# One gate-weight transfer, the last rows in column halves, adds and stores given to GpSimd: a change to the start and the end of a fused attention and gated-MLP kernel

## Chip, cores, metric

One core of a Trainium2 chip runs the kernel. The metric is the device time of one execution in microseconds. A figure quoted for a kernel is the median of its runs. The profile is of one execution, and its span is about 1.8 us shorter than that execution's time.

## The reference, cut to what matters

```python
xn = layernorm(A_x)                                  # 2048 rows of 640
q  = (xn @ wq) -> 32 heads of 192;  k, v = last 512 positions of the caches
s  = softmax(q k^T / sqrt(192)) v  -> 6144 columns;  s = s @ wo
g  = silu((sigmoid(xn @ w_gate) * (xn @ w_up)) @ w_down)
return A_x + s * g                                   # bf16, 2048 x 640
```

## The kernel before

The rows are taken in 4 blocks of 512, the heads in 8 groups of 4, so there are 32 units (a group and a block). At the start, the first block's tiles of 128 rows are normalised and transposed on TensorE while the first gate and up weights arrive. TensorE runs the matmuls of tile 0, with the transposes of tile 1 in the middle:

```python
load_x(0, 1)                                 # rows 0-127, sync queue
load_x(1, 1)
load_f(nc.scalar, wg_sb, wg_r, 0, 4, 0, 3)   # gate weights, piece 1 (384 KB), activation queue
load_f(nc.sync,   wg_sb, wg_r, 0, 4, 3, NCD) # gate weights, piece 2 (256 KB), sync queue
load_f(nc.scalar, wu_sb, wu_r, 0, 4, 0, 3)   # up weights, piece 1
load_x(2, 1)
load_f(nc.sync,   wu_sb, wu_r, 0, 4, 3, NCD)
load_x(3, 1)
```

At the end, the last group's projection of a row tile is multiplied by the gate `g`, added to the kept sum `acc` (which already holds `A_x` plus the other groups' part times `g`), and stored:

```python
for cc in range(GC):                         # 6 steps, 512 + 128 columns each
    for d0, d1 in ((0, 512), (512, D)):
        nc.tensor.matmul(wide(k)[:, d0:d1], ...)
if g == NG - 1:
    o_sb = fin.tile([P, D], F32, name="o_sb", bufs=2)
    nc.vector.tensor_tensor(o_sb[:], wide(k)[:, 0:D], gate[:, t, :], ALU.mult)
    r_sb = gate[:, t, :]
    parts = ((0, D),) if out_eng is not None else ((0, 384), (384, D))
    for i, (d0, d1) in enumerate(parts):
        nc.vector.tensor_tensor(r_sb[:, d0:d1], o_sb[:, d0:d1], acc[:, t, d0:d1], ALU.add)
        eng = out_eng or (nc.scalar, nc.sync)[i]
        eng.dma_start(of[t * P:(t + 1) * P, d0:d1], r_sb[:, d0:d1])
# ... the last units, u = NU - 2:
# project(u - 2, ...), project(u - 1, ...) with stores on nc.sync, between score matmuls
# values and transposes (by DMA, sync queue) of u and u + 1
# project(u, q, order[q], nc.sync);  project(u + 1, q, order[q], nc.scalar if q < 3 else None)
```

The softmax here doesn't subtract the row's maximum and nothing guards it: scores larger than these inputs give would overflow.

## Time and profile before

| | before |
|---|---|
| median of three runs | 928.17 us (927.81 to 928.33) |
| the profiled execution | 929.19 us, span 927.4 us |
| TensorE busy | 919.2 us, 99% |

The page's busy table and the chain that ended last, of the kernel before (the chain names, for each share of the span, the work that had to finish before the next could go on):

```profile
PE 919.2 (99%) x8004; PEld 547.2 (59%) x8004; DVE 467.2 (50%) x736; ACT 302.8 (33%) x333; POOL 126.0 (14%) x152
...
PE 97%; DMA 1%; DVE 1%; SPq 0%; issue 0%; ACT 0%; DVEq 0%; ACTq 0%
```

TensorE is the bound almost everywhere. What is not TensorE lies at the two ends. The timeline of the kernel before, at the start (columns: start in us, duration, engine, line, operation, output and inputs, count, and in brackets the idle time before it and what ended it):

```profile
6.29 1.16 PE L300 MATMUL bank<-xnT,wg_sb 128*128 128x128 bf16 x12
...
8.44 0.62 PE L300 MATMUL bank<-xnT,wg_sb 128*128 128x128 bf16 x8 [0.99 <-DMA wg_sb<-in_B_w_gate_dram]
9.29 0.49 DVE L198 BATCH_NORM_STATS2 st<-x_sb 128x6 f32<-128x320 bf16 x1 [2.22 <-DMA x_sb<-in_A_x_dram]
...
9.50 0.84 PE L300 MATMUL bank<-xnT,wu_sb 128*128 128x128 bf16 x12 [0.44 <-DMA wu_sb<-in_B_w_up_dram]
...
10.19 0.45 PE L230 MATMUL bank<-ident,xn 128*128 128x128 bf16 x5
```

Twelve gate matmuls run on the first piece; TensorE then waits for the second, and again for the up weights. The transposes of the second tile (L230) mark the end of this load-bound stretch. The timeline of the kernel before, at the end:

```profile
908.67 1.79 PE L457 MATMUL bank<-wo_last,oT 128*128 128x512 bf16 x12
...
911.03 11.58 PE L457 MATMUL bank<-wo_last,oT 128*128 128x512 bf16 x84 [0.57 <-DMA oT<-o_st]
...
922.13 0.83 DVE L466 TENSOR_TENSOR gate<-o_sb,acc 128x640 bf16<-128x640 f32 x1
922.87 0.82 DVE L461 TENSOR_TENSOR o_sb<-bank,gate 128x640 f32<-128x640 f32 x1
923.79 0.90 DVE L466 TENSOR_TENSOR gate<-o_sb,acc 128x384 bf16<-128x384 f32 x2
924.71 0.33 SPq L468 DMA_DIRECT2D out_dram<-gate  x1
```

The chain of waits at the start, of the same trace, goes through the first up piece and the matmuls that use it:

```profile
1.68 7.78 DMA wu_sb<-in_B_w_up_dram
...
9.50 0.84 PE bank L300 x12
```

At the end, the second row tile waits 0.57 us for its transpose. VectorE needs 0.82 us to multiply and 0.83 us to add a row, against 1.63 us of TensorE work.

### The profile page before, as it was taken

To read this page: it belongs to the slowest core of one execution; us is meant where nothing else is said; L and a number is where in the kernel's file an instruction comes from. 1 tells how busy PE (TensorE), PEld (TensorE's weight loads), DVE (VectorE), ACT (ScalarE), POOL (GpSimd) and SP (SyncE) were. 2 spreads that over 40 slices of the span, in tenths; PEclk is the share of its full clock that TensorE was granted. 3 is DMA by queue.
4 is the path that set the end of the run, shared out by engine and by line. 5 is a ranking of instruction groups with operands and counts; after the bars stand their busy time and mean duration, and the time that the engine had idled before them with its cause. 6 is when DMAs were issued, how large, how long until landed. Compare 5 with 4: busy or idle time off the path is not lost.

```text
span 927.4 us, 18043 instructions
## 1 busy us (share of the span) xinstructions
PE 919.2 (99%) x8004; PEld 547.2 (59%) x8004; DVE 467.2 (50%) x736; ACT 302.8 (33%) x333; POOL 126.0 (14%) x152
## 2 busy tenths in 40 slices
PE   8999999999999999999999999999999999999997
PEld 6445454465756565656565656566666656565665
DVE  5452522444645464545454555545554545454567
ACT  3222222255141424242423333332324242415240
POOL 1000110001002000200020011001100110175720
PEclk9999999999999999999999999999999999999999
DMA  9310340115424233333424152415251515253625
GB/s 318 80 22 8 88 86 1 43 60 87 82 58 111 78 69 70 97 92 41 97 87 103 39 99 78 111 35 104 65 111 40 110 61 98 66 115 96 102 74 125
DMA packets 162686, 76.68 MB, mean 83 GB/s; under 512 B 140944, under 2 KB 158176, under 8 KB 162608
## 3 DMA queue, kind: packets, MB, share of 16 engines
q1 hardware_dynamic: 155424, 53.64, 27.1%
q0 software_dynamic: 5808, 20.52, 7.9%
q8 instruction: 62, 1.02, 0.5%
q10 hardware_dynamic: 1376, 1.38, 0.4%
q14 instruction: 16, 0.13, 0.1%
HBM read 39.45 MB, written 2.62 MB: 45 GB/s over the span
## 4 chain that ended last, share of the span: by engine, by line
PE 97%; DMA 1%; DVE 1%; SPq 0%; issue 0%; ACT 0%; DVEq 0%; ACTq 0%
PE bank L457 21%; PE bank L421 21%; PE bank L437 18%; PE bank L403 18%; PE bank L250 10%; PE bank L262 6%; PE bank L369 1%; DMA wu_sb<-in_B_w_up_dram 1%; PE bank L300 1%; DVE gate L466 1%; DVE o_sb L461 1%; DMA oT<-o_st 1%; SPq L449 0%; PE bank L230 0%; ACT xnT L236 0%
## 5 line engine op out<-in xcount | busy, mean ns | idle before, releaser
L407 ACT ACTIVATE E<-bank 128x1024 bf16<-128x1024 f32 x256 | 255.8, 1024 | 456.8 <-PE bank L403 456.6
L421 PE MATMUL bank<-xnT,wq_sb 64*128 64x512 bf16 x1800 | 223.7, 376 | 0.0
L457 PE MATMUL bank<-wo_sb,oT 128*128 128x512 bf16 x1344 | 200.8, 299 | 0.0
L403 PE MATMUL bank<-qT,kT 64*128 64x512 bf16 x1536 | 198.4, 376 | 0.0
L437 PE MATMUL bank<-vbuf,E 128*128 128x193 bf16 x2048 | 189.5, 247 | 0.0
L437 PEld LDWEIGHTS <-E 128*128 128x128 bf16 x2048 | 168.6, 98 | 18.0 <-issue 6.4
L428 DVE CAST qT<-bank 128x1024 bf16<-128x1024 f32 x90 | 110.2, 1225 | 128.5 <-PE bank L421 128.5
L457 PEld LDWEIGHTS <-oT 128*128 128x128 bf16 x1536 | 121.0, 98 | 79.0 <-issue 1.3
L421 PEld LDWEIGHTS <-wq_sb 64*128 64x128 bf16 x1800 | 93.1, 100 | 102.2
L403 PEld LDWEIGHTS <-kT 64*128 64x128 bf16 x1536 | 74.0, 94 | 89.8 <-issue 4.8
L443 DVE TENSOR_TENSOR o_st<-bank,rden 128x768 bf16<-128x768 f32 x128 | 122.6, 958 | 4.4
L472 DVE TENSOR_TENSOR acc<-bank,acc 128x640 f32<-128x640 f32 x96 | 79.2, 825 | 43.3 <-PE bank L457 43.2
L118 POOL DMA_DIRECT2D vbuf<-in_A_v_cache_dram x28 | 21.1, 755 | 306.9 <-PE bank L437 304.0
L426 DVE COPY seen<-bank 128x2 f32<-128x2 f32 x90 | 14.4, 160 | 93.8 <-PE bank L421 93.8
L442 DVE RECIPROCAL rden<-bank 128x4 f32<-128x4 f32 x128 | 23.4, 183 | 65.1 <-PE bank L437 65.1
L250 PE MATMUL bank<-xnT,wu_sb 128*128 128x512 bf16 x220 | 54.7, 379 | 0.0
L250 PE MATMUL bank<-xnT,wg_sb 128*128 128x512 bf16 x220 | 54.7, 379 | 0.0
L262 PE MATMUL bank<-wd_sb,hT 128*128 128x512 bf16 (+1 forms) x384 | 52.8, 299 | 0.0
L256 DVE TENSOR_TENSOR hT<-bank,sig 128x512 bf16<-128x512 f32 x44 | 30.3, 690 | 43.7 <-ACT sig L253 43.7
L253 ACT ACTIVATE sig<-bank 128x512 bf16<-128x512 f32 x44 | 26.3, 597 | 68.4 <-PE bank L250 65.2
L262 PEld LDWEIGHTS <-hT 128*128 128x128 bf16 x384 | 29.7, 98 | 23.1
L250 PEld LDWEIGHTS <-wu_sb 128*128 128x128 bf16 x220 | 21.5, 98 | 26.0
(51 smaller groups left out, 317.7 us busy)
## 6 DMA issues: line engine op xcount, KB each, us to landing
wo_sb<-in_A_wo_dram SPq DMA_DIRECT2D x7, 960.0 KB, 5.3
wq_sb<-in_A_wq_dram POOLq DMA_DIRECT2D x7, 960.0 KB, 6.0
k_st<-in_A_k_cache_dram POOLq DMA_DIRECT2D x14, 384.0 KB, 5.2
vbuf<-in_A_v_cache_dram POOLq DMA_DIRECT2D x28, 192.0 KB, 3.3
row<-in_A_x_dram POOLq DMA_DIRECT2D x16, 160.0 KB, 2.8
oT<-o_st SPq DMA_TRANSPOSE x128, 2.6
x_sb<-in_A_x_dram SPq DMA_DIRECT2D x3, 640.0 KB, 9.4
wd_sb<-in_B_w_down_dram SPq DMA_DIRECT2D x1, 1920.0 KB, 12.9
```

What stands on the lines that cost most here:

```text
L250: nc.tensor.matmul(bank[k][:, half, 0:r1 - r0], lhsT=w[:, c, f * P:(f + 1) * P], rhs=xnT[:, b, c, r0:r1], start=(c == 0), stop=(c == NCD - 1))
L253: nc.scalar.activation(sig[:, 0:r1 - r0], bank[k][:, 0, 0:r1 - r0], AF.Sigmoid)
L256: nc.vector.tensor_tensor(hT[b][:, f, r0:r1], bank[k][:, 1, 0:r1 - r0], sig[:, 0:r1 - r0], ALU.mult)
L262: nc.tensor.matmul(wide(k)[:, d0:d1], lhsT=hT[b][:, f, q * P:(q + 1) * P], rhs=wd_sb[:, f, d0:d1], start=(f == 0), stop=(f == NF - 1))
L403: nc.tensor.matmul(bank[k][:, i, :], lhsT=kT[r, pr, j, c * P:(c + 1) * P], rhs=q[r, pr * DJ + j, :], start=(j == 0), stop=(j == DJ - 1))
L407: nc.scalar.activation(E[u, pr][:, c, :, :], bank[k][:], AF.Exp, scale=scale_qk)
L421: nc.tensor.matmul(bank[k][:, half, :], lhsT=wq[r, c, col:col + DJ * (P - 1) + 1:DJ], rhs=xnT[r, b, c, :], start=(c == 0 and not second), ...
L428: nc.vector.tensor_copy(qT[u][:, 2 * m:2 * m + 2, :], bank[k][:])
L437: nc.tensor.matmul(o4[:, q, 0:DH + 1], lhsT=e[:, c, h % 2, q * P:(q + 1) * P], rhs=vbuf[:, h, c, 0:DH + 1], start=(c == 0), stop=(c == KC ...
L443: nc.vector.tensor_tensor(o_st[u][:, :, h * DH:(h + 1) * DH], o4[:, :, 0:DH], rden[:].to_broadcast([P, TQ, DH]), ALU.mult)
L457: nc.tensor.matmul(wide(k)[:, d0:d1], lhsT=oT[u][:, cc, q * P:(q + 1) * P], rhs=wo[:, cc, d0:d1], start=(cc == 0), stop=(cc == GC - 1))
L472: nc.vector.tensor_tensor(acc[:, t, :], wide(k)[:, 0:D], acc[:, t, :], ALU.add)
```

## The change

The intent: fewer transfers before the first gate matmuls; smaller last pieces for VectorE; half of VectorE's last work on the otherwise idle GpSimd; and a sync queue that is free of stores before the last transposes.

```diff
-        load_f(nc.scalar, wg_sb, wg_r, 0, 4, 0, 3)
-        load_f(nc.sync, wg_sb, wg_r, 0, 4, 3, NCD)
-        load_f(nc.scalar, wu_sb, wu_r, 0, 4, 0, 3)
+        load_f(nc.scalar, wg_sb, wg_r, 0, 4)
+        load_f(nc.sync, wu_sb, wu_r, 0, 4, 0, 3)
 ...
+    def finish_rows(t, d0, d1, src, add, out_eng):
+        o_sb = fin.tile([P, D], F32, name="o_sb", bufs=2)[:, d0:d1]
+        r_sb = gate[:, t, d0:d1]
+        nc.vector.tensor_tensor(o_sb, src, r_sb, ALU.mult)
+        add.tensor_tensor(r_sb, o_sb, acc[:, t, d0:d1], ALU.add)
+        out_eng.dma_start(of[t * P:(t + 1) * P, d0:d1], r_sb)
 ...
+        if u == NU - 1:
+            HD = D // 2
+            for i in range(2):
+                for cc in range(GC):
+                    nc.tensor.matmul(bank[k[i]][:, 0, 0:HD], ...)
+                finish_rows(t, i * HD, (i + 1) * HD, bank[k[i]][:, 0, 0:HD], add, out_eng[i])
+            return
 ...
-        project(u - 2, ..., nc.sync)      # and u - 1: eight stores
+        project(u - 2, ..., nc.gpsimd)
 ...
-        project(u, q, order[q], nc.sync)
+        project(u, q, order[q], nc.sync, nc.gpsimd if q < 3 else nc.vector)
 ...
-        project(u + 1, q, order[q], nc.scalar if q < 3 else None)
+        i = 2 * q % 4
+        project(u + 1, q, order[i:i + 2], (nc.scalar, nc.sync), nc.gpsimd if q < 3 else nc.vector)
```

So there are three independent parts: the head (one gate transfer), the store move, and the tail (column halves with GpSimd adds).

More of the change, by code (lines that the diff above doesn't have):

```diff
@@ L449, in turn_out, with project @@
             nc.sync.dma_start_transpose(oT[u][:, :, q * P:(q + 1) * P], o_st[u][:, q, :])
-    def project(u, q, k, out_eng):
+    def finish_rows(t, d0, d1, src, add, out_eng):
[4 more added lines that the diff above has]
+        out_eng.dma_start(of[t * P:(t + 1) * P, d0:d1], r_sb)
+    def project(u, q, k, out_eng, add=nc.vector):
         g, b = u // NB, u % NB
@@ L454, in project @@
         t = b * TQ + q
+        if u == NU - 1:
+            HD = D // 2
+            for i in range(2):
+                for cc in range(GC):
+                    nc.tensor.matmul(bank[k[i]][:, 0, 0:HD],
+                                     lhsT=oT[u][:, cc, q * P:(q + 1) * P],
+                                     rhs=wo[:, cc, i * HD:(i + 1) * HD],
+                                     start=(cc == 0), stop=(cc == GC - 1))
+                finish_rows(t, i * HD, (i + 1) * HD, bank[k[i]][:, 0, 0:HD], add, out_eng[i])
+            return
         for cc in range(GC):
@@ L459, in project @@
         if g == NG - 1:
-            o_sb = fin.tile([P, D], F32, name="o_sb", bufs=2)
-            nc.vector.tensor_tensor(o_sb[:], wide(k)[:, 0:D], gate[:, t, :], ALU.mult)
-            r_sb = gate[:, t, :]
-            parts = ((0, D),) if out_eng is not None else ((0, 384), (384, D))
-            for i, (d0, d1) in enumerate(parts):
-                nc.vector.tensor_tensor(r_sb[:, d0:d1], o_sb[:, d0:d1], acc[:, t, d0:d1], ALU.add)
-                eng = out_eng or (nc.scalar, nc.sync)[i]
-                eng.dma_start(of[t * P:(t + 1) * P, d0:d1], r_sb[:, d0:d1])
+            finish_rows(t, 0, D, wide(k)[:, 0:D], add, out_eng)
         elif g == 0:
@@ L517 @@
     for q in range(2):
-        project(u - 2, q, q, nc.sync)
+        project(u - 2, q, q, nc.gpsimd)
     for i in range(6, 12):
@@ L521 @@
     for q in range(2, 4):
-        project(u - 2, q, q - 2, nc.sync)
+        project(u - 2, q, q - 2, nc.gpsimd)
     for i in range(12, 16):
@@ L525 @@
     for q in range(4):
-        project(u - 1, q, order[q], nc.sync)
+        project(u - 1, q, order[q], nc.gpsimd)
     for v in (u, u + 1):
```

## The prediction

> **What bounds the kernel.** TensorE is busy 99% of the 927.4 us span (the page's busy table); the chain of waits puts 97% on it. Only three places are not TensorE work: the load-bound start up to about 11.2 us, a 4.94 us transpose near 906 us (TensorE idle 0.57), and the end after TensorE's last matmul. The change leaves the matmul count alone, so 20 to 880 us should be unchanged. At stake are about 5 us; 2% is 18.6. The answer is "same".
>
> **The start** (timeline, 0 to 12 us). Gate weights come in two transfers: twelve gate matmuls run at 6.29 us, TensorE waits 0.99 us for the second piece (8.44), then 0.44 us for the first up-weights (9.50). The token-tile transposes at 10.19 wait for the third row load (first use 9.29), not for gate weights. With one 640 KB transfer all twenty gate matmuls (about 1.15 us warm) begin when the whole has landed. The bytes ahead of the third row load are the same in total; TensorE's clock went full at 6.97 us, and idling from 6.5 to 8.2 should not cool it. I estimate the gate block landing at 7.6 to 8.4 and the transposes at 10.1 to 10.4 again: 0 us, between -0.4 and +0.4.
>
> **The end** (timeline, 904 to 927.4). Before, VectorE is the tail: from 912.87 it runs seven rows, each a multiply (0.82) and an add (0.83), 1.67 us per row, back to back, against TensorE's 1.63. Its last add ends at 924.69, the matmuls about 922.6; then 2.7 us of closing.
> Removed: six rows' adds from VectorE. Column halves cost TensorE nothing (2 x 320 columns streams as 512 + 128; twelve weight loads in both). Ideally the last half needs two operations of 0.48 (estimated from 0.82 for 640 columns) after 922.65: ending near 923.7, 1.0 us earlier.
> But GpSimd takes 1.39 to 1.41 us for a 640-column two-input operation here[...]. A half is some 0.72 us, barely under TensorE's 0.82. The scratch has two buffers, so each multiply waits for the GpSimd add two halves earlier, and VectorE starts the first half late (about 917.9), doing the fourth row's add itself. GpSimd then runs behind and returns the last scratches at about 922.1 and 922.9. VectorE's add also has two SBUF inputs[...] (an add of 1.09 instead of 0.83 us beside GpSimd at 888.25). I put VectorE's end near 924.3: 0.4 us saved, between 0.9 saved and 0.2 lost.
>
> **Stores by GpSimd:** issued by about 901 us, before the transposes at 904.8; the sync queue was idle before those. Nothing gained; the 4.94 us transpose coincides with an instruction fetch and stays.
>
> **Sum.** 928.17 - 0.0 - 0.4 = about 927.7 us; range 926.6 to 928.7. Faster by over 2%: 0.5%; within 2%: 99%; slower: 0.5%.
>
> **Right or wrong.** First gate matmul after 7.5 us without the 0.99 us gap, second tile's matmuls again near 11.2; no change from 20 to 880; in the tail VectorE idle, waiting for TensorE and GpSimd, GpSimd halves near 0.72 us, VectorE ending 0 to 0.9 us earlier.
>
> **What would make it wrong.** A cold TensorE clock at the start (up to +1.2 us); GpSimd halves over 0.85 us, making GpSimd the tail; a gate transfer landing much earlier (-0.5); a moved instruction fetch changing the transpose wait (0.6 us).

## The result

The changed kernel took 927.61 us (927.18 to 929.13, four runs), the one before 928.18 us. Ratios here are the mean time of one kernel's fast runs over that of the other's of the same rounds, so they are not quite the ratio of the medians quoted: 0.9997, 95% interval 0.998 to 1.0015. It is "same", and the predicted 927.7 us is met. But 0.6 us can be the sum of larger terms of both signs, so the two traces are read piece by piece.

The start, timeline of the changed kernel:

```profile
8.08 1.29 PE L299 MATMUL bank<-xnT,wg_sb 128*128 128x128 bf16 x20 [1.87 <-DMA wg_sb<-in_B_w_gate_dram]
8.35 0.49 DVE L197 BATCH_NORM_STATS2 st<-x_sb 128x6 f32<-128x320 bf16 x1 [1.24 <-DMA x_sb<-in_A_x_dram]
...
9.21 0.83 PE L299 MATMUL bank<-xnT,wu_sb 128*128 128x128 bf16 x12
...
9.88 0.44 PE L229 MATMUL bank<-ident,xn 128*128 128x128 bf16 x5
```

All twenty gate matmuls run at once, later, at the full clock (granted clock 1.00, 1.29 us for twenty); the third row load comes 0.94 us earlier, and the transposes 0.31 us earlier. The end:

```profile
908.76 6.69 PE L475 MATMUL bank<-wo_last,oT 128*128 128x512 bf16 x47 [0.25 <-DVE rden L441]
...
911.51 3.17 POOL L455 TENSOR_TENSOR gate<-o_sb,acc 128x640 bf16<-128x640 f32 x2 [10.87 <-DVE o_sb L454]
...
914.84 1.54 POOL L455 TENSOR_TENSOR gate<-o_sb,acc 128x640 bf16<-128x640 f32 x1 [0.15 <-DVE o_sb L454]
...
915.29 6.68 PE L467 MATMUL bank<-wo_last,oT 128*128 128x320 bf16 x48
...
917.73 4.97 POOL L455 TENSOR_TENSOR gate<-o_sb,acc 128x320 bf16<-128x320 f32 x6 [1.35 <-DVE o_sb L454]
...
921.10 0.49 DVE L454 TENSOR_TENSOR o_sb<-bank,gate 128x320 f32<-128x320 f32 x1 [0.33 <-POOL gate L455]
921.91 0.49 DVE L454 TENSOR_TENSOR o_sb<-bank,gate 128x320 f32<-128x320 f32 x1 [0.33 <-POOL gate L455]
922.44 0.61 DVE L455 TENSOR_TENSOR gate<-o_sb,acc 128x320 bf16<-128x320 f32 x1
922.97 0.48 DVE L454 TENSOR_TENSOR o_sb<-bank,gate 128x320 f32<-128x320 f32 x1
923.49 0.49 DVE L455 TENSOR_TENSOR gate<-o_sb,acc 128x320 bf16<-128x320 f32 x1
```

The wait for the second transpose has gone, and one of 0.25 us before the first row has come. GpSimd's six half adds fill 917.73 to 922.70 without a gap. They start every 0.82 us, which is TensorE's own pace for a half (48 matmuls, six a half, in 6.68 us, against 6.69 for four whole rows), so GpSimd never makes up for its late start. One multiply of a half waits 0.58 us and four wait 0.33 us for GpSimd to give a scratch buffer back: the waits of this stretch put it first among VectorE's waits that TensorE does not cause (time in all, times, longest).

```profile
DVE o_sb L454 <- POOL gate L455: 1.9, 5, 0.6
```

VectorE ends at 923.98. TensorE's last matmul starts at 921.68, so VectorE ends 2.30 us after it. Before it was 2.29. Taking most of the adds off VectorE has gained nothing there.

Then comes a stretch that the chain does not show, because closing instructions do not count as work. These are the records of the closing in the two traces (read from the trace; us):

```
                                           before    changed
VectorE's last add ends                    924.69     923.98
last store's landing counted               926.27     925.59
sync engine ready (its drain starts)       926.66     925.86
GpSimd's last operation ends               888.66     922.70
GpSimd's drain ends                        891.85     926.55
GpSimd opens the closing barrier           926.69     926.60
```

(A drain is an instruction of the closing that the traces record on each engine before the barrier at which the engines wait for each other; in the changed kernel it takes 0.01 us on the sync engine, 0.15 on ScalarE, 0.53 on VectorE, 2.02 on TensorE and 4.92 on GpSimd. GpSimd's began at 921.63, before its last add was over, and ended at 926.55.) In the kernel before, GpSimd's drain is over 35 us before the end, and the closing follows the last store. In the changed one, the drain ends 3.85 us after GpSimd's last add, and the closing waits for it, about 0.7 us after the sync engine, with the stores done, is ready. That gives the first theory:

**Theory A.** The head and the store move gain; the tail loses, because GpSimd's last add is followed by a drain of over 3 us, and because VectorE's end does not move. **Rivals:** the head's gain is chance; the drain is only a shadow of the profile; VectorE's last add decides the time, so the tail gains whatever it gains there; the stores have no effect.

### The profile page after: what moved, and what is told of

Read it like the earlier page. It is cut to its first block, busy times and chain, and to the rows that moved or that the text cites. A ratio compares the mean times of both kernels' runs of the same rounds, so it can differ in the third digit from the quotient of the medians.

```text
span 927.3 us, 17975 instructions
## 1 busy us (share of the span) xinstructions
PE 914.2 (99%) x7926; PEld 547.5 (59%) x8004; DVE 464.0 (50%) x734; ACT 302.5 (33%) x333; POOL 140.0 (15%) x169
## 3 DMA queue, kind: packets, MB, share of 16 engines
q8 instruction: 62, 1.02, 0.5%
## 4 chain that ended last, share of the span: by engine, by line
PE 97%; DMA 1%; issue 1%; POOL 0%; DVE 0%; ACT 0%; DVEq 0%
PE bank L475 22%; PE bank L420 21%; PE bank L436 19%; PE bank L402 18%; PE bank L249 10%; PE bank L261 6%; PE bank L368 1%; PE bank L299 1%; DMA wg_sb<-in_B_w_gate_dram 1%; POOL gate L455 0%; DVE o_sb L454 0%; PE bank L229 0%; DVE gate L455 0%; ACT xnT L235 0%; DVE warm L165 0%
## 5 line engine op out<-in xcount | busy, mean ns | idle before, releaser
L475 PE MATMUL bank<-wo_sb,oT 128*128 128x512 bf16 (+1 forms) x1288 | 197.9, 296 | 2.9
L475 PEld LDWEIGHTS <-oT 128*128 128x128 bf16 x1488 | 117.3, 98 | 75.8 <-issue 1.3
L261 PE MATMUL bank<-wd_sb,hT 128*128 128x128 bf16 (+1 forms) x376 | 52.4, 297 | 0.4
L97 POOL DMA_DIRECT2D wq_sb<-in_A_wq_dram x7 | 6.3, 899 | 221.0 <-PE bank L420 221.0
```

Source lines behind the costliest of these rows:

```text
L261: nc.tensor.matmul(wide(k)[:, d0:d1], lhsT=hT[b][:, f, q * P:(q + 1) * P], rhs=wd_sb[:, f, d0:d1], start=(f == 0), stop=(f == NF - 1))
L475: nc.tensor.matmul(wide(k)[:, d0:d1], lhsT=oT[u][:, cc, q * P:(q + 1) * P], rhs=wo[:, cc, d0:d1], start=(cc == 0), stop=(cc == GC - 1))
```

## The experiments

Each ran five rounds, in three batches, each batch on one chip beside the kernel before. Every variant's result was correct. The middle can be taken out of the comparison: from the second tile's transposes to the start of the last 128 value matmuls, every trace has 887.8 us (before: 898.00 - 10.19 = 887.81; changed: 897.68 - 9.88 = 887.80). So three intervals describe a run: T, the start of the second tile's transposes; M, from the first of those value matmuls to the start of the last matmul; and C, from there to the closing (the first of GpSimd's short drains after the barrier opens). All are in us, worked out from each run's one trace. "V" is VectorE's end after the last matmul starts.

| run | median | before in its batch | ratio (95%) | T | M | V | C |
|---|---|---|---|---|---|---|---|
| before | 928.17 | | | 10.19 | 24.40 | 2.29 | 4.46 |
| changed | 927.61 | 928.18 | 0.9997 (0.9980-1.0015) | 9.88 | 24.00 | 2.30 | 5.09 |
| changed, again | 927.56 | 928.07 | 0.9994 (0.9981-1.0006) | 8.57 | 24.05 | 2.29 | 5.08 |
| head only | 927.49 | 928.07 | 0.9995 (0.9983-1.0008) | 8.51 | 24.26 | 2.29 | 4.54 |
| changed, old head | 928.53 | 928.07 | 1.0007 (0.9995-1.0020) | 9.56 | 23.57 | 2.28 | 5.07 |
| before + late GpSimd op | 929.34 | 928.07 | 1.0013 (0.9999-1.0027) | 9.94 | 24.41 | 2.29 | 5.75 |
| adds on VectorE | 928.08 | 928.09 | 1.0001 (0.9987-1.0014) | 8.64 | 24.01 | 3.38 | 5.44 |
| six scratch halves | 927.89 | 928.09 | 0.9996 (0.9984-1.0009) | 8.51 | 23.81 | 1.67 | 5.39 |
| bf16 adds on VectorE | 926.26 | 928.09 | 0.9979 (0.9967-0.9992) | 8.47 | 23.81 | 1.60 | 3.68 |
| stores only | 927.73 | 928.09 | 0.9996 (0.9984-1.0009) | 9.22 | 23.65 | 2.31 | 4.49 |
| gate pieces, one queue | 928.34 | 928.53 | 0.9998 (0.9985-1.0012) | 8.87 | 24.39 | 2.27 | 4.44 |
| head + stores | 927.15 | 928.53 | 0.9987 (0.9975-1.0000) | 8.26 | 24.20 | 2.31 | 4.54 |
| bf16, whole rows | 926.37 | 928.53 | 0.9981 (0.9968-0.9993) | 9.23 | 23.65 | 1.72 | 4.00 |
| bf16, whole rows, pieces | 927.32 | 928.53 | 0.9989 (0.9977-1.0002) | 9.64 | 23.63 | 1.72 | 3.90 |

Most intervals include 1: five rounds don't settle a difference of some tenths by time alone. V and C repeat to about 0.1 us between runs with the same code in that place, and they carry the argument about the tail. T varies from run to run by more than 1 us with the same code, and M by up to 0.6 us (the changed tail has 24.00, 24.05 and 23.57); what goes with that is said under "Stores only". It also warns about the first pair of traces: the profiled executions of before (929.19) and of the changed kernel (929.13) were each above the other runs of their kernel, with late starts.

### The changed kernel again

> The changed kernel unaltered, as the control of its batch. The three unprofiled-looking runs so far (927.2 to 927.7) lie 0.6 us under the kernel before (928.2), the profiled one 0.06 us under the profiled one of before. Theory A (gains at the start and in the tail are real, about 0.6 to 0.7 us, and partly eaten by GpSimd's closing drain): ratio to before 0.9992 to 0.9996, about 0.5 us. Theory B (no real difference): ratio within 0.9998 to 1.0002.

It took 927.56 us, 0.51 under before, as theory A had it by the medians; the ratio (0.9994) lies in its range too, but by time alone the interval still includes 1. T was 8.57 instead of 9.88, C the same to 0.01 us.

### Head only

```diff
 (kernel before)
-        load_f(nc.scalar, wg_sb, wg_r, 0, 4, 0, 3)
-        load_f(nc.sync, wg_sb, wg_r, 0, 4, 3, NCD)
-        load_f(nc.scalar, wu_sb, wu_r, 0, 4, 0, 3)
+        load_f(nc.scalar, wg_sb, wg_r, 0, 4)
+        load_f(nc.sync, wu_sb, wu_r, 0, 4, 0, 3)
```

> The kernel before with only the gate weights' single transfer. Theory A: second token tile's first gate matmul at 10.9 instead of 11.2 us, and the whole 0.3 us kept up to TensorE's last matmul unless the transposes near 906 us absorb it: 0.2 to 0.4 us faster than before. Rival (the head's gain is chance[...], or is absorbed by the waits for the transposes near 906 us): within 0.1 us of before.

It took 927.49 us, 0.58 under before by the medians: by itself it has as much as the whole change gains, and more than was expected. Its interval includes 1; the next experiment is the clearer test. The start of its timeline:

```profile
6.50 1.29 PE L299 MATMUL bank<-xnT,wg_sb 128*128 128x128 bf16 x20 [0.46 <-DMA wg_sb<-in_B_w_gate_dram]
...
7.61 0.49 DVE L197 BATCH_NORM_STATS2 st<-x_sb 128x6 f32<-128x320 bf16 x1 [0.77 <-DMA x_sb<-in_A_x_dram]
7.62 0.83 PE L299 MATMUL bank<-xnT,wu_sb 128*128 128x128 bf16 x12
...
8.51 0.45 PE L229 MATMUL bank<-ident,xn 128*128 128x128 bf16 x5
```

The whole gate block is there at 6.45 us, hardly later than the old first piece is used (6.29), and the third row load at 7.59 instead of 9.27. The landings show what was late. In the traces the semaphore of each of these loads gets sixteen counts, and the engine that waits for the load starts just after the sixteenth. In the trace of before, fifteen counts of the second gate piece came by 6.80 us and the sixteenth at 8.39 (its matmuls start at 8.44); of the first up piece, 7.43 and 9.46 (9.50); of the third row load, 7.73 and 9.27 (its statistics start at 9.29). The last count came 1.5 to 2.0 us after the fifteenth, and all three waits lasted until it came. In the head-only trace the same row load had 7.37 and 7.59.

It is not always a single late count. In the trace of stores only, also with pieces on two queues, the fifteenth and sixteenth of the row load come together (8.25 and 8.30), but 1.1 us after the median count. Over all traces, the last count of the row load comes 1.1 to 2.1 us after the median one with the pieces on two queues (four traces), and with one transfer 0.1 to 0.4 us after it in six traces and 1.1 in two. One of these two is the first trace of the changed kernel, where the gate block had 5.82 and 8.03, which is why that start looked almost like the old one.

Nor is the row load alone what the transposes wait for. It acts through VectorE, which takes the statistics of the third tile before it normalises the second. In the four traces with the old head this path and the one through the first up piece end within 0.1 us of each other; in the first trace of the changed kernel the gate block decides; in the other seven with one transfer it is the row load. Over all traces, T is 9.73 on average with the pieces on two queues (four traces, 9.22 to 10.19) and 8.76 with one transfer (eight traces, 8.26 to 9.88).

### The changed kernel with the old head

```diff
 (changed kernel)
-        load_f(nc.scalar, wg_sb, wg_r, 0, 4)
-        load_f(nc.sync, wu_sb, wu_r, 0, 4, 0, 3)
+        load_f(nc.scalar, wg_sb, wg_r, 0, 4, 0, 3)
+        load_f(nc.sync, wg_sb, wg_r, 0, 4, 3, NCD)
+        load_f(nc.scalar, wu_sb, wu_r, 0, 4, 0, 3)
```

> The changed kernel with the old start (gate weights in two transfers). Theory A: loses the start's 0.3 us and keeps the tail: VectorE's last add about 1.3 to 1.5 us after TensorE's last matmul begins its drain instead of 2.1, closing held by GpSimd's drain; 0.1 to 0.4 us faster than before, 0.3 slower than the changed kernel. Rival (all of the gain came from the tail): as fast as the changed kernel.

It took 928.53 us, 0.46 slower than before and 0.97 slower than the changed kernel. This is a miss: a small gain was expected, and VectorE was to end sooner, but V is 2.28 as before. The rival, that all of the gain is in the tail, falls. It is also the cleanest test of the head: in the same batch, with all else equal, the five runs of the changed kernel (927.17 to 927.85) all lie below the five with the old head (928.35 to 929.85). So the head's gain is hardly chance. Against before, from M and C one would have expected about 0.2 us faster at the same T (M 0.83 less, C 0.61 more); the rest is not settled.

### The kernel before, with one late GpSimd operation

```diff
 (kernel before, after the last project)
+    nc.gpsimd.tensor_tensor(mhalf[:], mhalf[:], gate[:, NT - 1, 0:1], ALU.add)
```

> The kernel before with one added GpSimd operation of one column that reads the last row's result, so GpSimd finishes last. In both traces so far GpSimd's drain ends 3.2 to 3.9 us after its last operation. Drain theory: GpSimd's last operation ends near 924.8, its drain near 928.0 to 928.6, where the closing began at 926.7 in the kernel before: 1.3 to 2.0 us slower, 929.5 to 930.2 us. Rival (the drain's length is spent idle and shortens when it matters, or exists only in the profile): within 0.2 us of before.

It took 929.34 us, 1.27 slower than before, just under the 1.3 to 2.0 that was expected. Almost nothing was added to the work; the timeline of its end:

```profile
923.53 0.90 DVE L466 TENSOR_TENSOR gate<-o_sb,acc 128x384 bf16<-128x384 f32 x2
924.17 0.30 POOL L535 TENSOR_TENSOR mhalf<-mhalf,gate 128x1 f32<-128x1 f32 x1 [35.83 <-DVE gate L466]
924.46 0.33 SPq L468 DMA_DIRECT2D out_dram<-gate  x1
```

GpSimd's drain ended at 927.67, 3.20 us after the operation's end at 924.48. The sync engine had been ready at 926.39, and the barrier opened at 927.72: 1.3 us of waiting, much as in the medians. The drain is real, it takes over 3 us after GpSimd's last work, and by an estimate from these times (3.2 to 3.85 us of drain, against 0.3 to 0.4 us from the last landing to the sync engine's readiness) it counts when that work ends less than about 3 us before the last store has landed. The rival, that it exists only in the profile, falls: the interval just includes 1, but all five runs (929.09 to 930.23) lie above all nine of before (927.60 to 929.04).

### All adds on VectorE

```diff
 (changed kernel)
-        project(u, q, order[q], nc.sync, nc.gpsimd if q < 3 else nc.vector)
+        project(u, q, order[q], nc.sync)
-        project(u + 1, ..., (nc.scalar, nc.sync), nc.gpsimd if q < 3 else nc.vector)
+        project(u + 1, ..., (nc.scalar, nc.sync))
```

> The changed kernel with all its adds on VectorE: halves and stores as changed, GpSimd idle at the end. Theory A (splitting rows in halves without help makes VectorE the tail: a half costs about 1.03 us there, a full row 1.67, against TensorE's 0.82 and 1.63): VectorE ends about 3.5 us after TensorE's last matmul starts, instead of 2.3; GpSimd's drain is long over; in total 0.8 to 1.3 us slower than the changed kernel, 0.3 to 0.8 slower than before. Rival (GpSimd's part is worth nothing, its drain costs what it saves): within 0.2 us of the changed kernel.

It took 928.08 us, equal to before, about 0.5 slower than the changed kernel (of another batch, whose before was 928.07). Theory A expected 0.8 to 1.3 slower, and 0.3 to 0.8 slower than before; both sizes were missed. V is 3.38, about as expected (3.5): halves alone make VectorE the tail. From its timeline:

```profile
921.83 0.48 DVE L454 TENSOR_TENSOR o_sb<-bank,gate 128x320 f32<-128x320 f32 x1
922.42 0.49 DVE L455 TENSOR_TENSOR gate<-o_sb,acc 128x320 bf16<-128x320 f32 x1
922.82 0.48 DVE L454 TENSOR_TENSOR o_sb<-bank,gate 128x320 f32<-128x320 f32 x1
923.34 0.49 DVE L455 TENSOR_TENSOR gate<-o_sb,acc 128x320 bf16<-128x320 f32 x1
```

A half costs 0.93 or 1.00 us in turn from multiply to multiply (expected: 1.03), where TensorE needs 0.82. The add of a half takes 0.49 us, more than half of a row's 0.83: an estimate from these two is a fixed part of about 0.49 x 2 - 0.83 = 0.15 us an add. The closing no longer waits for GpSimd, so C (5.44) exceeds the changed kernel's (5.08) by only 0.36 though V is worse by 1.09.

### Six scratch halves

```diff
 (changed kernel, in finish_rows, for the six halves that GpSimd adds)
-        o_sb = fin.tile([P, D], F32, name="o_sb", bufs=2)[:, d0:d1]
+        o_sb = flat[:, n * D:(n + 1) * D].bitcast(F32)     # flat: a dead score buffer, n = 0..5
```

A first version with four ordinary buffers did not fit into memory and ran nowhere (the build asks for 12.5 KB a partition where 9.8 are left).

> The changed kernel with six separate scratch halves in a dead buffer for the last unit's halves that GpSimd adds, so that no multiply waits for GpSimd. Theory A (GpSimd's drain, about 3.85 us after its last add, holds the closing): VectorE ends 0.5 to 0.9 us sooner after TensorE than in the changed kernel, its waits for GpSimd gone, but GpSimd still ends about 1.0 us after TensorE's last matmul starts, and the total is the same within 0.2 us. Rival (VectorE's last add sets the total): 0.5 to 0.9 us faster.

It took 927.89 us, 0.20 under before in its batch and no faster than the changed kernel. VectorE's waits for GpSimd were gone (they now name TensorE), and VectorE ended 1.67 us after the last matmul started, 0.63 sooner than in the changed kernel. But GpSimd ended 1.33 us after it instead of 1.02, its drain 3.85 us later, and the closing waited for that: C is 5.39. Against the changed kernel of the other batch it is 0.33 slower, a little more than the 0.2 that theory A allowed. GpSimd's six adds, back to back again, in the timeline:

```profile
916.25 5.21 POOL L463 TENSOR_TENSOR gate<-E,acc 128x320 bf16<-128x320 f32 x6 [1.42 <-DVE E L462]
```

VectorE's last add does not set the time here; GpSimd's end and its drain do.

### bf16 adds on VectorE

```diff
 (variant with all adds on VectorE)
-            nc.gpsimd.tensor_tensor(acc[:, t, :], acc[:, t, :], x_sb[:], ALU.add)
+            nc.gpsimd.tensor_tensor(acc16(t), acc[:, t, :], x_sb[:], ALU.add)
+    def acc16(t): return acc[:, t, 0:D // 2].bitcast(BF16)    # the sum in place, as bf16
-        o_sb = fin.tile([P, D], F32, name="o_sb", bufs=2)[:, d0:d1]
+        o_sb = fin.tile([P, D], BF16, name="o_sb", bufs=2)[:, d0:d1]
-        add.tensor_tensor(r_sb, o_sb, acc[:, t, d0:d1], ALU.add)
+        add.tensor_tensor(r_sb, o_sb, acc16(t)[:, d0:d1], ALU.add)
```

GpSimd writes the finished sum as bf16 over 35 us before the end, which costs nothing there (these adds take 1.39 to 1.40 us, against 1.39 in the trace of before); the output is bf16 anyway, and the result was correct.

> The changed kernel with all adds on VectorE, and scratch and the kept sum in bf16, which should let an add of two bf16 inputs run in about 0.4 us a row instead of 0.83 (0.25 to 0.32 a half). Theory A: VectorE keeps up with TensorE, ends 1.2 to 1.6 us after TensorE's last matmul starts (2.3 in the changed kernel), GpSimd's drain is over long before: 0.8 to 1.4 us faster than the changed kernel. Rival (bf16 changes nothing in the add's time): as slow as the variant with all adds on VectorE.

It took 926.26 us, 1.83 under before: the fastest of all, its interval clear of 1. Every run of it (925.71 to 926.56) is below every run of the variant with all adds on VectorE (927.65 to 928.98) of the same batch, and C differs by as much as V does (1.76 and 1.78). From its timeline:

```profile
914.84 0.49 DVE L458 TENSOR_TENSOR gate<-o_sb,acc 128x640 bf16<-128x640 bf16 x1
...
920.61 0.33 DVE L458 TENSOR_TENSOR gate<-o_sb,acc 128x320 bf16<-128x320 bf16 x1
920.85 0.48 DVE L457 TENSOR_TENSOR o_sb<-bank,gate 128x320 bf16<-128x320 f32 x1
921.37 0.33 DVE L458 TENSOR_TENSOR gate<-o_sb,acc 128x320 bf16<-128x320 bf16 x1
```

The add of a row takes 0.49 us instead of 0.83 (0.4, my estimate, was expected), of a half 0.33 instead of 0.49. By an estimate as above, the fixed part is about 0.33 x 2 - 0.49 = 0.17 us, and the rest of a row's add 0.32 us with two bf16 inputs, where it is 0.68 (0.83 - 0.15) with two fp32 inputs. V is 1.60 and C 3.68: VectorE nearly keeps up with TensorE by itself, and GpSimd's last add is long over.

### Stores only

```diff
 (kernel before)
-        project(u - 2, ..., nc.sync)      # and u - 1
+        project(u - 2, ..., nc.gpsimd)
```

> The kernel before with only the eight stores of the two earlier units moved to GpSimd. Theory: they end before the transposes near 904 us in either kernel, and GpSimd's drain is over long before the end: within 0.2 us of before. Rival (stores on the sync queue delay the transposes): 0.3 to 0.6 us faster, with a shorter wait of TensorE near 910 us.

It took 927.73 us, 0.36 under before: the rival's size and not the theory's, though the interval includes 1. The reason that the rival gave does not fit the trace: in that of before the last of these stores ends at 902 us, and the first transpose is issued at 904.8. What differs in the trace is an instruction fetch. The transfers of the kernel before, 9.0 to 14.5 us after the value matmuls start, by queue (packets, MB, share of the 16 engines):

```profile
q1 hardware_dynamic: 2400, 0.59, 92.5%
q8 instruction: 1, 0.02, 1.9%
q14 instruction: 1, 0.01, 0.4%
```

The same stretch of the variant:

```profile
q1 hardware_dynamic: 2702, 0.67, 80.9%
q8 instruction: 1, 0.02, 1.4%
```

The 8 KB fetch of the second instruction queue falls 11.6 to 11.8 us after the value matmuls start in the four traces with sync stores in which I looked for it (before, head only, the late GpSimd operation, the pieces on one queue). In all ten traces with GpSimd stores it falls between 20.4 and 20.8 us, clear of the first transposes. M is 24.26 to 24.41 in those four and 23.57 to 24.20 in all ten with GpSimd stores (23.84 on average). So the gain in M differs: with the single transfer it is only 0.06 us between head only (24.26) and head + stores (24.20).

The ten fall into two groups by the other fetch, of 16 KB. In four (changed, changed again, adds on VectorE, head + stores) it starts 8.7 to 8.9 us after the value matmuls start, the first transpose lands at 11.0 to 11.2 instead of 9.3 us, TensorE waits 0.25 to 0.38 us for it, and M is 24.00 to 24.20. In the other six it starts at 9.05 to 9.1, the second transpose is the late one, TensorE does not wait, and M is 23.57 to 23.81. In the four traces with sync stores it starts at 9.1 too, so the six are the fair comparison: there the second transpose lands 0.65 us after the sync engine has issued the third, in the four with sync stores 1.11 to 1.14 us after it, with the 8 KB fetch in between. Why the 16 KB fetch moves is open. That the sync engine's shorter program moves the 8 KB fetch is my reading and was not shown; that the fetch delays the transpose is argued from their meeting in time. Neither was taken away by itself.

### Gate pieces on one queue

```diff
 (kernel before)
-        load_f(nc.sync, wg_sb, wg_r, 0, 4, 3, NCD)
-        load_f(nc.scalar, wu_sb, wu_r, 0, 4, 0, 3)
+        load_f(nc.scalar, wg_sb, wg_r, 0, 4, 3, NCD)
+        load_f(nc.sync, wu_sb, wu_r, 0, 4, 0, 3)
```

> The kernel before with the gate weights still in two pieces, but both on the activation queue, and the first up-weights on the sync queue. Queue theory[...]: the lag shrinks as with the single transfer, the transposes of the second token tile start near 8.5 us, and the run is as fast as the head alone, 0.4 to 0.8 us under before. Rival (it is the size of the transfer, fewer and larger, that matters): as slow as before, transposes at 9.2 to 10.2.

The queue theory is that the counts of a load fall far apart when pieces come by two queues. It took 928.34 us, 0.19 under before. T was 8.87 here and 9.64 in the last variant below, between the two ranges. It decides for neither theory: why the last counts lag, and why the single transfer mostly avoids it, stays open.

### Head and stores, without the tail

```diff
 (stores only)
-        load_f(nc.scalar, wg_sb, wg_r, 0, 4, 0, 3)
-        load_f(nc.sync, wg_sb, wg_r, 0, 4, 3, NCD)
-        load_f(nc.scalar, wu_sb, wu_r, 0, 4, 0, 3)
+        load_f(nc.scalar, wg_sb, wg_r, 0, 4)
+        load_f(nc.sync, wu_sb, wu_r, 0, 4, 0, 3)
```

> The kernel before with the single gate transfer and the eight GpSimd stores, but no column halves and no GpSimd adds. If the parts add (head about -0.6, stores about -0.35, halves with GpSimd adds about +0.5 to +0.8): about 927.1 us, 0.3 to 0.6 us faster than the whole change. Rival (halves and GpSimd adds are worth nothing or help): as fast as the whole change, 927.5, or slower.

It took 927.15 us, 1.38 under before of its batch, and 0.41 under the changed kernel (of another batch). Taken each against before in its own batch, the two differ by 0.87 (1.38 and 0.51). So two of the three parts, without the third, look better than all three; the sizes are not settled by time, and this trace has the earliest T of all (8.26). The closing, which repeats, says the same: C is 4.54 against 5.08, 0.54 us.

### bf16 adds with whole rows

```diff
 (bf16 adds on VectorE)
-        if u == NU - 1:
+        if u == NU - 1 and q == 3:       # only the last row in halves
```

> The variant with bf16 adds on VectorE, but whole rows except for the last, which is done in two halves. In the variant with halves throughout a half costs VectorE 0.82 to 0.84 us, just over TensorE's 0.82, and it ends 1.6 us after TensorE's last matmul starts. Expected here: a row costs VectorE about 1.35 us against 1.63, so it waits for TensorE and ends 1.15 to 1.3 us after the last matmul starts; 0.2 to 0.5 us under the variant with halves, near 925.9 us. Rival (stores or the closing set the end): no faster than 926.2.

It took 926.37 us, no faster than with halves (its interval, too, is clear of 1), and V was 1.72 instead of 1.15 to 1.3: a miss. The 0.82 to 0.84 us of the expectation was not right either: in the trace with halves throughout, multiplies of halves start 0.76 and 0.83 us apart in turn, 0.80 on average, so VectorE did keep pace there. The timeline shows the step that I had left out:

```profile
919.40 0.82 DVE L457 TENSOR_TENSOR o_sb<-bank,gate 128x640 bf16<-128x640 f32 x1 [0.21 <-PE bank L479]
920.33 0.49 DVE L458 TENSOR_TENSOR gate<-o_sb,acc 128x640 bf16<-128x640 bf16 x1
920.74 0.48 DVE L457 TENSOR_TENSOR o_sb<-bank,gate 128x320 bf16<-128x320 f32 x1
```

VectorE has time to spare, but the third row's multiply cannot start before the whole row is done (919.40), so its add still runs when the last row's first half is complete, and both halves come late. The same with the gate weights in two pieces on one queue:

> The same with the gate weights in two pieces on the activation queue. If the queue theory holds, as fast as with the single transfer or up to 0.3 us faster, since twelve gate matmuls can run before the second piece is there; if it fails, 0.5 to 0.8 us slower.

It took 927.32 us, 0.95 slower than with one transfer, with T at 9.64: two pieces are not better, even on one queue.

## Why the prediction was right, and where it was not

The time (927.7 predicted, 927.61 measured) and "same" were right. That is luck: the sum was right because its terms were wrong in both directions.

- **The start: "0 us, between -0.4 and +0.4".** This step failed. The head gained 0.58 us alone, and 0.97 between the changed kernel and the one with the old head. I had the transposes wait for the third row load alone, counted the bytes in front of it and found them equal. In the trace of before they wait as much for the first up piece (landed at 9.46), and both loads were held by a last count that came 1.5 to 2.0 us after the fifteenth; why it was late stays open. With one transfer the last counts mostly come together and T is 0.97 us earlier on average. The prediction named an early landing of the gate block as something that would make it wrong (-0.5), and that is what seven of the eight traces with one transfer show (5.75 to 6.96 us, where 7.6 to 8.4 was predicted). The first trace of the changed kernel, with the first gate matmul at 8.08 us, looked like a confirmation and was the exception. The clock stayed at its full value, as said: the trace of the changed kernel has it granted in full from 5.70 us to the end, and the twenty matmuls after 1.87 us of idling took 1.29 us. In the trace of before that record starts at 6.97 us: up to 6.9 us matmuls of 128 columns start every 0.106 us, from 7.0 us on every 0.056, so by an estimate from these two, twenty at the slower pace would take 1.0 us longer (1.2 was allowed for).
- **The end: "0.4 us saved".** This step failed. VectorE's end after the last matmul did not move (2.29 and 2.30 us). The mechanism named was right: GpSimd ran behind and handed its buffers back late. Its size was off: a half took 0.87 us, one every 0.82, not the 0.72 of my estimate, so it could not catch up with TensorE's 0.82. By an estimate from 1.54 us for a row and 0.87 for a half, GpSimd has a fixed part of 0.20 us, and an add of two fp32 inputs is slower there (1.54 us a row, where 1.39 to 1.42 was measured with one bf16 input, but for one operation of 1.77 us in before and one of 2.06 in the changed kernel). That this goes with the inputs and not with the bf16 output is seen in the variant with bf16 adds, where GpSimd's adds with one bf16 input and a bf16 output take 1.39 to 1.40 us. An add of VectorE beside one of GpSimd's took longer, as the prediction had it: 0.61 us instead of 0.49 at 922.44, while GpSimd runs until 922.70 (in before, a row's add took 1.09 instead of 0.83 at 888.25, while GpSimd runs until 888.65; beside the one at 882.55 it was GpSimd's that took longer, 1.77 instead of 1.39). That GpSimd's reads are the cause is argued from their meeting in time, not shown.
- **What the prediction did not have: GpSimd's drain.** It ends 3.20 to 3.85 us after GpSimd's last operation and holds the closing. C grew from 4.46 to 5.09 us. Together the tail (halves and GpSimd adds) costs about 0.5 to 0.6 us by C, and 0.4 to 0.9 by the medians, where 0.4 was to be saved.
- **The stores: "Nothing gained".** This failed too, as far as five rounds can tell: stores alone were 0.36 us under before (the interval includes 1), with M shorter by about 0.5 us on average over the traces. There are two instruction fetches near the transposes; I took them as fixed, and the second moved away. That this is the cause is argued, not shown.
- **20 to 880 us: unchanged.** Right, to 0.01 us.

With T's averages (-0.97), M's (-0.53) and C's difference (+0.59: 5.08 against 4.49, the averages of the traces with the changed tail and with the old one), the traces would give -0.9 us for the whole change; the medians give -0.5 to -0.6. The interval of the changed kernel against before (0.9981 to 1.0006) holds both.

## What to carry to other kernels

Work given to an idle engine near the end of a kernel is not free because the engine is idle: ask when that engine is finished, drain included (here 3.20 to 3.85 us after its last operation), and compare it with the landing of the last store. Before handing half of a tail to a slower engine, look whether the first engine can do it faster: two 16-bit inputs (0.49 us for a row's add instead of 0.83) did here what GpSimd could not, and gave the best version (926.26 us). And when a change of several parts moves the time by its noise, run the parts alone: here a part that gained was paying for one that lost.
